# Seven quarter products in place of eight in the second dense layer of the last three token blocks

## The chip, the core and the metric

The kernel runs on one core of one Trainium2 chip. A core has TensorE (matmuls, called PE in the profile; its weight loads are shown apart as PEld), VectorE (DVE), ScalarE (ACT), GpSimd (POOL) and SyncE (SP, which here only issues transfers). [...] Each engine runs its instructions in the order in which they stand in its queue, and waits on semaphores for the others. The metric is the device time of one run of the program in microseconds (us), the median of several runs.

## What is computed

Local and pooled attention over 8 batches of 576 tokens with 8 heads of 64, whose sum is the input x (4608 x 512) of a two-layer block:

```python
def _moe_ref(x, w_in, w_out) -> np.ndarray:
    h = x @ w_in               # 4608 x 512 by 512 x 2048
    g = h - np.tanh(h)
    return (g @ w_out).astype(np.float32)   # 4608 x 2048 by 2048 x 512
```

The attention part, cut: `q`, `k`, `v` are averaged over groups of 4 tokens, attended among themselves and repeated 4 times; to this is added an attention of each token to the tokens less than 4 away; the heads are then joined to the 512 columns of x. The change touches only the last matrix product.

## The kernel before

The attention works on 32 pairs of heads (8 batches of 4 pairs). For each pair q and k are loaded (`qkn`), cast and reordered (`qr`, L408), transposed (`qk`), pooled on GpSimd (`half` L449, `qkd` L454), multiplied to scores (L468 and L484), put through the exponential (`E`, L501 to L514), masked on VectorE (L504, L517), multiplied with v (L528, L535), normalized (`ln`, L546) and transposed back into `xT`, four tiles of 128 x 4608 bf16, one for each 128 columns of x (L572 and L578 for the later batches: the join, on VectorE or GpSimd).

The dense layers work on 9 blocks of 512 tokens. `mm1(kb, fc)` makes one of the 16 groups of 128 hidden columns of block kb: four matmuls of 512 columns (L609) into one of four PSUM slots `ps_hy`, tanh on ScalarE into `u` (L617), the subtraction on VectorE into `gT` (L620, 128 x 16 x 512 bf16, two buffers). `mm2(kb, i)` makes a quarter of an output tile of 128 tokens: four matmuls of 512 columns (L636) with `gT` as the stationary and `w_out_sb` as the moving operand, 16 matmuls for a tile, in the same four PSUM slots. After each fourth call the tile is copied to `y` by ScalarE (L647) and stored by SP (L650, 256 KB). `dense(kb)` interleaves the calls: one `mm1` of block kb, one `mm2` of block kb-1. The last call, `dense(9)`, has only `mm2` of block 8.

The order of work is not that of the program text. Every operation is recorded with its engine, a duration in ns, the keys that it reads and writes, and a priority (a lower number goes first); `Program.order` then plays the program through with these durations and writes each engine's queue in the order of the planned starts. Attention has priorities around 10 times the pair number, tanh, subtraction and copies have -1, the matmuls of the dense layers 5000, so these fill TensorE where attention leaves room. Some operations (casts, pooling, joins) may go to one of several engines and are given to the one that is free first. The real waits are set from the accesses in the resulting order, so the order is fixed while the run's timing is not. In the last part, from about 240 us, attention is over and TensorE has only dense matmuls.

Of the kernel before, what the change touches and what calls it, by code (L numbers as in the profile page):

```python
# [8 lines left out]
FP32 = mybir.dt.float32  # L9
BF16 = mybir.dt.bfloat16  # L10
AF = mybir.ActivationFunctionType
ALU = mybir.AluOpType
# [3 lines left out]
class Program:  # L16
# [18 lines left out]
    def op(self, eng, ns, fn, reads=(), writes=(), pri=0):  # L35
        i = len(self.ops)
        deps = set()
        for key in reads:
            if key in self.last_write:
                deps.add(self.last_write[key])  # L40
        for key in writes:
            if key in self.last_write:
                deps.add(self.last_write[key])
            deps.update(self.readers.get(key, ()))
        for key in reads:
            self.readers.setdefault(key, set()).add(i)
# [104 lines left out]
def kernel(  # L151
# [9 lines left out]
    nc = tc.nc  # L161
    B, H, S, D = q.shape
    Dm, Dff = moe_w_in.shape
# [9 lines left out]
    NT = 5  # L173
    NQ = [120, 120, 120, 120, 96]
    KOFF = 585
    N_FF = Dff // 128
# [6 lines left out]
    def fixed(name, shape, dt, n=None, pool=const):  # L183
        if n is None:
            return pool.tile(shape, dt, name=name, tag=name)
        return [pool.tile(shape, dt, name=f"{name}{i}", tag=f"{name}{i}")
                for i in range(n)]

    NQKN, NVST, NVW = 4, 5, 3
# [4 lines left out]
    xT = [fixed(f"xT{j}", [128, NTOK], BF16) for j in range(NP)]  # L194
    w_in_sb = fixed("w_in_sb", [128, N_DC, Dff], BF16)
    w_out_sb = fixed("w_out_sb", [128, N_FF, Dm], BF16)
    qkn = fixed("qkn", [128, 2, A9 * D], FP32, NQKN)
    vst = fixed("vst", [128, 2, NT, 64], FP32, NVST)
    vw = fixed("vw", [128, 4, NT, 65], BF16, NVW)
    vd = fixed("vd", [128, 2, 4, 65], BF16, NVW)  # L200
    qr = fixed("qr", [128, A9, 128], BF16, 2)
# [2 lines left out]
    half = fixed("half", [128, 2, G, 2], FP32)  # L204
# [7 lines left out]
    r = fixed("r", [128, 2, 7], FP32, 2)  # L212
    ln = fixed("ln", [128, 7, 128], BF16, 2)
    od = fixed("od", [128, G], BF16, 2)
    gT = fixed("gT", [128, N_FF, 512], BF16, 2)
# [3 lines left out]
    ps_ts = fixed("ps_ts", [128, 2, 512], FP32, pool=psum)  # L219
    ps_ox = fixed("ps_ox", [128, 2, 512], FP32, pool=psum)  # L220
# [14 lines left out]
    op = P.op  # L235
    V, A, T, GP = nc.vector, nc.scalar, nc.tensor, nc.gpsimd
# [362 lines left out]
    def mm1(kb, fc):  # L599
        slot, us, g = hy[0] % 4, un[0] % 3, kb % 2  # L600
        hy[0] += 1
        un[0] += 1
        bs = sorted({kb * 512 // S, (kb * 512 + 511) // S})

        def mm(part):
            if not ps_hy:
                dense_banks()
            for dc in range(2 * part, 2 * part + 2):
                T.matmul(ps_hy[slot], w_in_sb[:, dc, fc * 128:(fc + 1) * 128],  # L609
                         xT[dc][:, kb * 512:kb * 512 + 512],  # L610
                         start=(dc == 0), stop=(dc == N_DC - 1))
        for part in range(2):
            op("PE", 432, lambda part=part: mm(part),
               reads=[("w_in", fc // 4, c) for c in range(4)] +
               [("x", b, j) for b in bs for j in range(NP)],
               writes=[("hy", slot)], pri=5000)
        op("ACT", 490, lambda: A.activation(  # L617
            out=u[us], in_=ps_hy[slot], func=AF.Tanh),
           reads=[("hy", slot)], writes=[("u", us)], pri=-1)
        op("DVE", 620, lambda: V.tensor_tensor(  # L620
            out=gT[g][:, fc, :], in0=ps_hy[slot], in1=u[us], op=ALU.subtract),
           reads=[("hy", slot), ("u", us)], writes=[("gT", g, fc)], pri=-1)
# [4 lines left out]
    def mm2(kb, i):  # L627
        ts, part, g = i // 4, i % 4, kb % 2
        if part == 0:
            ycur[0] = hy[0] % 4  # L630
            hy[0] += 1
        slot = ycur[0]

        def mm(e):
            for fc in range(4 * part + 2 * e, 4 * part + 2 * e + 2):
                T.matmul(ps_hy[slot], gT[g][:, fc, ts * 128:ts * 128 + 128],  # L636
                         w_out_sb[:, fc, :],
                         start=(fc == 0), stop=(fc == N_FF - 1))
        for e in range(2):
            op("PE", 432, lambda e=e: mm(e),  # L640
               reads=[("w_out", part, c) for c in range(4)] +
               [("gT", g, fc) for fc in range(4 * part, 4 * part + 4)],
               writes=[("hy", slot)], pri=5000)
        if part == 3:
            ys = yn[0] % 3
            yn[0] += 1
            op("ACT", 490, lambda: A.copy(out=y[ys], in_=ps_hy[slot]),  # L647
               reads=[("hy", slot)], writes=[("y", ys)], pri=-1)
            r0 = kb * 512 + ts * 128
            op("SP", 600, lambda: nc.sync.dma_start(  # L650
                out=out[r0:r0 + 128, :], in_=y[ys]),
               reads=[("y", ys)], writes=[("yq", ys)], pri=-1)
            op("DMA", 1000, None, reads=[("yq", ys), ("y", ys)], pri=-1)

    def dense(kb):

        if kb == 0:
            for i in range(16):
                mm1(kb, i)
            for i in range(M2_FIRST):  # L660
                mm2(kb, i)
            return
        if kb == 1:
            for i in range(16):
                mm1(kb, i)
                if M2_FIRST + i < 16:
                    mm2(0, M2_FIRST + i)
            return
        for i in range(16):
            if kb < NBLK:  # L670
                mm1(kb, i)
            mm2(kb - 1, i)


    M2_FIRST, T_DMA, X_DMA, NEW = 16, 16, 16, 16
# [13 lines left out]
    for i in range(2):  # L689
        def guards(i=i):  # L690
# [3 lines left out]
           writes=[("qk", i, a) for a in range(2)])  # L694
    for i in range(NVW):
        def ones(i=i):
# [3 lines left out]
           writes=[("vd", i), ("vw", i, 0), ("vw", i, 1)])  # L700
        op("POOL", 200, lambda i=i: GP.affine_select(
            out=vd[i][:, 1, :, 64], in_=vd[i][:, 1, :, 64], compare_op=ALU.is_ge,
            fill=0.0, base=-112, pattern=[[0, 4]], channel_multiplier=1),
           writes=[("vd", i)], pri=-96)
    for i in range(2):
        op("DVE", 70, lambda i=i: V.memset(E[i][:, 1728:1840], 0.0),
           writes=[("E", i, 2)], pri=-94)
# [24 lines left out]
    for i in range(2):  # L732
        op("DVE", 70, lambda i=i: V.memset(qkd[i][:, 288:344], 0.0),
           writes=[("qkd", i)], pri=-94)
        op("DVE", 70, lambda i=i: V.memset(vp[i][:, :, :, 64:65], 4.0),
           writes=[("vp", i)], pri=-94)
# [28 lines left out]

    ctx.enter_context(tc.manual_schedule())
# [38 lines left out]
```

## Time and profile before

| | |
|---|---|
| time, median of 3 runs | 343.2 us (343.11 to 343.61) |
| span of the profiled execution | 345.0 us |
| L609, first layer, 576 matmuls of 128x512 | 146.9 us busy |
| L636, second layer, 576 matmuls of 128x512 | 142.7 us busy |
| L620, subtraction on VectorE, 144 | 96.6 us busy, 686 ns each |
| L617, tanh on ScalarE, 144 | 83.9 us busy, 598 ns each |
| L647, copy of an output tile on ScalarE, 36 | 21.2 us busy, 588 ns each |

The profile is of one execution; its span is 1.8 us longer than the median of the timed runs, and every sum made from it is made against 345.0. Busy times of different engines overlap. The busy time of a matmul group is the time in which at least one of them is in flight; the mean duration of one (379 ns) is longer than the distance between two starts, since they are pipelined.

### The profile page before, as it was taken

What the parts mean: (1) busy time and instruction counts of PE and PEld (TensorE: products, weight loads), DVE (VectorE), ACT (ScalarE), POOL (GpSimd) and SP (SyncE); (2) the same over time, 40 slices, a digit from 0 to 9 for tenths busy, and PEclk for the clock granted to TensorE, in tenths of its full rate; (3) what the DMA queues carried; (4) which work ended last, traced back from release to release, by engine and by line L of the source; (5) the groups of instructions that cost most, each with busy time, mean ns of one, the idle gap of its engine ahead of it and who ended that gap; (6) DMA issues with size and microseconds to landing.
All of it is one profiled execution on the core that took longest, in us unless ns stands there. A gap on an engine that the chain in (4) does not pass through costs nothing.

```text
span 345.0 us, 6688 instructions
## 1 busy us (share of the span) xinstructions
PE 326.0 (94%) x2498; PEld 164.2 (48%) x2498; DVE 220.7 (64%) x365; ACT 220.5 (64%) x353; POOL 152.6 (44%) x196
## 2 busy tenths in 40 slices
PE   4978959999999999999899999999999999999995
PEld 1554435555555554444454444544444444444442
DVE  3687747667999977889789777876333433343300
ACT  3775836658997888979878877974443444344411
POOL 5762224555558747987877688462000000000000
PEclk9599989999999999999999999999999999999999
DMA  7999999779869976999999999723001000100021
GB/s 209 240 230 228 206 301 301 195 227 281 219 149 214 244 203 155 246 232 282 233 210 256 234 251 224 105 67 86 30 30 63 30 30 32 61 30 32 31 91 62
DMA packets 99214, 56.52 MB, mean 164 GB/s; under 512 B 77678, under 2 KB 86382, under 8 KB 99182
## 3 DMA queue, kind: packets, MB, share of 16 engines
q1 hardware_dynamic: 94958, 51.91, 61.2%
q0 software_dynamic: 4224, 4.19, 7.3%
q8 instruction: 19, 0.31, 0.4%
q14 instruction: 13, 0.11, 0.1%
HBM read 42.46 MB, written 9.44 MB: 150 GB/s over the span
## 4 chain that ended last, share of the span: by engine, by line
PE 72%; DMA 11%; DVE 4%; ACT 4%; POOL 3%; issue 3%; SPq 1%; POOLq 0%; ACTq 0%; DVEq 0%
PE ps_hy L636 30%; PE ps_hy L609 29%; DMA qkn<-in_k_dram 9%; PE ps_ts L468 3%; PE ps_ox L528 3%; DMA qkn<-in_q_dram 2%; PE ps_ts L433 2%; ACT qk L424 2%; PE ps_ox L535 2%; DVE E L504 2%; PE ps_ox L560 1%; POOL half L449 1%; DVE gT L620 1%; DVE qr L408 1%; POOL v L364 1%
## 5 line engine op out<-in xcount | busy, mean ns | idle before, releaser
L609 PE MATMUL ps_hy<-xT,w_in_sb 128*128 128x512 bf16 x576 | 146.9, 382 | 1.4 <-DVE xT L589 0.9
L636 PE MATMUL ps_hy<-w_out_sb,gT 128*128 128x512 bf16 x576 | 142.7, 379 | 0.0
L620 DVE TENSOR_TENSOR gT<-ps_hy,u 128x512 bf16<-128x512 f32 x144 | 96.6, 686 | 71.4 <-ACT u L617 70.8
L617 ACT ACTIVATE u<-ps_hy 128x512 f32<-128x512 f32 x144 | 83.9, 598 | 69.3 <-PE ps_hy L609 66.7
L636 PEld LDWEIGHTS <-gT 128*128 128x128 bf16 x576 | 54.6, 98 | 63.2
L609 PEld LDWEIGHTS <-w_in_sb 128*128 128x128 bf16 x576 | 53.0, 98 | 61.1 <-issue 3.6
L449 POOL TENSOR_TENSOR half<-qk 128x576 f32<-128x576 bf16 x29 | 33.4, 1151 | 36.9 <-ACT qk L437 26.0
L424 ACT COPY qk<-qT 128x576 bf16<-128x576 bf16 x32 | 37.8, 1206 | 0.0
L546 DVE TENSOR_TENSOR ln<-ps_ox,r 128x896 bf16<-128x896 f32 x32 | 34.9, 1090 | 1.1 <-DVE r L544 0.2
L501 ACT ACTIVATE E<-ps_ts 128x960 bf16<-128x960 f32 x32 | 31.0, 973 | 6.7 <-PE ps_ts L468 6.4
L504 DVE TENSOR_TENSOR E<-E,mask 128x960 bf16<-128x960 bf16 x32 | 28.4, 889 | 10.0 <-ACT E L501 9.7
L647 ACT COPY y<-ps_hy 128x512 f32<-128x512 f32 x36 | 21.2, 588 | 17.0 <-PE ps_hy L636 16.8
L408 DVE CAST qr<-qkn 128x576 bf16<-128x576 f32 x32 | 23.6, 738 | 8.3 <-DMA qkn<-in_k_dram 8.3
L408 POOL CAST qr<-qkn 128x576 bf16<-128x576 f32 x30 | 21.9, 730 | 15.7 <-DMA qkn<-in_k_dram 9.1
L343 POOL CAST vw<-vst 128x640 bf16<-128x640 f32 x30 | 25.3, 844 | 5.8 <-DMA vst<-in_v_dram 5.8
L437 ACT COPY qk<-ps_ts 128x1152 bf16<-128x1152 bf16 x16 | 18.0, 1125 | 10.8 <-PE ps_ts L433 10.5
L528 PE MATMUL ps_ox<-vw,E 128*128 128x65 bf16 x320 | 21.0, 196 | 2.1 <-DVE E L504 0.9
L454 POOL TENSOR_TENSOR qkd<-half 128x288 bf16<-128x288 f32 x30 | 21.2, 705 | 3.6 <-DVE r L544 2.4
L528 PEld LDWEIGHTS <-E 128*128 128x128 bf16 x320 | 17.0, 99 | 9.3 <-DVE E L517 1.4
L364 POOL TENSOR_TENSOR v<-v 72x512 f32<-72x512 f32 x16 | 20.7, 1296 | 0.6
L468 PEld LDWEIGHTS <-qk 64*128 64x128 bf16 x320 | 9.9, 97 | 17.5 <-issue 15.3
L368 POOL TENSOR_TENSOR vp<-v 72x256 bf16<-72x256 f32 x16 | 11.6, 728 | 14.1 <-PE ps_ox L535 14.0
(71 smaller groups left out, 250.0 us busy)
## 6 DMA issues: line engine op xcount, KB each, us to landing
vst<-in_v_dram SPq DMA_DIRECT2D x62, 160.0 KB, 5.2
qkn<-in_q_dram SPq DMA_DIRECT2D x32, 288.0 KB, 4.3
qkn<-in_k_dram SPq DMA_DIRECT2D x32, 288.0 KB, 4.5
out_dram<-y SPq DMA_DIRECT2D x36, 256.0 KB, 4.1
v<-in_v_dram SPq DMA_DIRECT2D x16, 288.0 KB
w_in_sb<-in_moe_w_in_dram POOLq DMA_DIRECT2D x4, 512.0 KB, 12.4
w_out_sb<-in_moe_w_out_dram POOLq DMA_DIRECT2D x4, 512.0 KB, 20.0
vst<-in_v_dram SPq DMA_DIRECT2D x2, 128.0 KB
```

What stands on the lines that cost most here:

```text
L343: P.choice([(eng, ns, lambda fn=fn: fn(out=vw[w][:, 2 * jj:2 * jj + 2, :, 0:64], in_=vst[s])) for eng, ns, fn in CAST_V[p >= NEARLY]], rea ...
L408: P.choice([(eng, ns, lambda dst=dst, srt=srt, fn=fn: fn(out=dst, in_=srt)) for eng, ns, fn in REORDER[p >= NEARLY][h]], reads=[("qkn", sn ...
L424: op("ACT", 600, lambda i=i: A.copy(out=full[:, i].rearrange("p (g a) -> p g a", a=A9), in_=qT[s].rearrange("p a (g i) -> p i g a", i=2)[: ...
L449: eng.tensor_tensor(out=half, in0=four[:, :, :, 0:2], in1=four[:, :, :, 2:4], op=ALU.add)
L501: op("ACT", 870, lambda: A.activation(out=e1, in_=ps[:, :, 0:480], func=AF.Exp, scale=SCALE), reads=ts, writes=[("E", s, 0)], pri=pri)
L504: op("DVE", 700, lambda: V.tensor_tensor(out=e1, in0=e1, in1=mask[:, 0:480].unsqueeze(1).to_broadcast([128, 2, 480]), op=ALU.mult), reads= ...
L528: T.matmul(po[:, hh, 65 * t:65 * t + 65], E[s][:, c:c + 128], vw[w][:, 2 * jj + hh, t, :], start=True, stop=True)
L546: op("DVE", 1010, lambda: V.tensor_tensor(out=ln[s].rearrange("p n (h d) -> p h n d", d=D), in0=blocks[:, :, :, 0:64], in1=r[s].unsqueeze( ...
L609: T.matmul(ps_hy[slot], w_in_sb[:, dc, fc * 128:(fc + 1) * 128], xT[dc][:, kb * 512:kb * 512 + 512], start=(dc == 0), stop=(dc == N_DC - 1))
L617: op("ACT", 490, lambda: A.activation(out=u[us], in_=ps_hy[slot], func=AF.Tanh), reads=[("hy", slot)], writes=[("u", us)], pri=-1)
L620: op("DVE", 620, lambda: V.tensor_tensor(out=gT[g][:, fc, :], in0=ps_hy[slot], in1=u[us], op=ALU.subtract), reads=[("hy", slot), ("u", us) ...
L636: T.matmul(ps_hy[slot], gT[g][:, fc, ts * 128:ts * 128 + 128], w_out_sb[:, fc, :], start=(fc == 0), stop=(fc == N_FF - 1))
```

## The change

For blocks 6, 7 and 8 (`KS = 6`) the product of g (512 tokens x 2048) and w_out (2048 x 512) is cut into quarters, A11 to A22 (256 tokens x 1024) and B11 to B22 (1024 x 256), and the four quarters of the output come from seven products of quarters in place of eight, by the Winograd form of Strassen's scheme. Each product is 16 matmuls of 256 columns (2 halves of 128 tokens, 8 groups of 128 hidden columns), in two steps of 8; a block has 112 of them where it had 64 matmuls of 512 columns.

- `weight_sums` (once, GpSimd, 16 operations of 128x512 bf16, priority 4000): T0 = B12-B11, T1 = B22-T0, T2 = B22-B12, T3 = B21-T1, written over columns 0 to 2047 of the four `xT` tiles, which the first layer has read by then.
- `token_sums` (each block, VectorE, 8 operations of 128x1024 bf16): S2 = A11-A21, S0 = A21+A22, S1 = S0-A11, S3 = A12-S1, written into the `qkn` tiles. The second half of S0 needs the last of the 16 groups of g.
- `phase`: product 1 (A11 B11) and, added into the same bank, 2 (A12 B21); 6 (S1 T1), 7 (S2 T2) and 4 (A22 T3) one after another in a second bank; 5 (S0 T0) and 3 (S3 B22) in a third. The three banks were those of the attention's scores and outputs (`ps_ts`, `ps_ox`). ScalarE copies the bank after 1, 2, 6 and 7 (a running sum, so the bank is not cleared in between); GpSimd adds the copy of 1 to the copies of 6 and 7 (128x512 f32); VectorE adds 5, 4 and 3 to the kept sums, from PSUM, into output tiles of 128 x 2 x 512 that lie over the `vst` buffers. The kept sums lie over `xT`, too.
- An output tile is a half block (256 tokens); its two stores of 256 KB leave together, after 4 and after 3.
- `dense`: in the loop of 16, each `mm1` is followed by one step of the products, in the program's order 1, 5, 6, 7, 2, 4, 3; the planner may move steps. In the planned order of the last block, where there is no first layer left, they stand as 1, 5, 6, 2, 7, 4, 3.
- The five `vst` buffers become slices of one tile of the same size.

```diff
--- before.py
+++ after.py
@@ -195,7 +195,9 @@
     w_in_sb = fixed("w_in_sb", [128, N_DC, Dff], BF16)
     w_out_sb = fixed("w_out_sb", [128, N_FF, Dm], BF16)
     qkn = fixed("qkn", [128, 2, A9 * D], FP32, NQKN)
-    vst = fixed("vst", [128, 2, NT, 64], FP32, NVST)
+    vst_all = fixed("vst", [128, NVST * 2 * NT * 64], FP32)
+    vst = [vst_all[:, 640 * i:640 * i + 640].rearrange("p (h t d) -> p h t d", h=2, t=NT)
+           for i in range(NVST)]
     vw = fixed("vw", [128, 4, NT, 65], BF16, NVW)
     vd = fixed("vd", [128, 2, 4, 65], BF16, NVW)
     qr = fixed("qr", [128, A9, 128], BF16, 2)
@@ -652,6 +654,170 @@
                reads=[("y", ys)], writes=[("yq", ys)], pri=-1)
             op("DMA", 1000, None, reads=[("yq", ys), ("y", ys)], pri=-1)
 
+    KS = 6
+    HB = N_FF // 2
+    HD = Dm // 2
+    bank = [ps_ts[:, 0, :], ps_ts[:, 1, :], ps_ox[:, 0, :]]
+    bkey = [("ts", 0), ("ts", 1), "ox"]
+    Sg = [qkn[i].rearrange("p i n -> p (i n)").bitcast(BF16)[:, 0:HB * 256]
+         .rearrange("p (f c) -> p f c", c=256) for i in range(4)]
+    Tw = [xT[j][:, 0:HB * HD].rearrange("p (f c) -> p f c", c=HD) for j in range(4)]
+    keep = [xT[j][:, 2048:3072].bitcast(FP32) for j in range(3)]
+    y2 = [vst_all[:, 1024 * i:1024 * i + 1024].rearrange("p (j c) -> p j c", j=2)
+          for i in range(3)]
+    tkeys = [("x", bb, j) for bb in range(4) for j in range(4)]
+    def weight_sums():
+        wq = w_out_sb.rearrange("p (r f) (c n) -> p r f c n", r=2, c=2)
+        b11, b12 = wq[:, 0, :, 0, :], wq[:, 0, :, 1, :]
+        b21, b22 = wq[:, 1, :, 0, :], wq[:, 1, :, 1, :]
+        wk = [("w_out", f, c) for f in range(4) for c in range(4)]
+        for n, (x0, x1, k0) in enumerate(((b12, b11, None), (b22, Tw[0], 0),
+                                          (b22, b12, None), (b21, Tw[1], 1))):
+            for e in range(4):
+                fs = slice(2 * e, 2 * e + 2)
+                def go(n=n, x0=x0, x1=x1, fs=fs):
+                    GP.tensor_tensor(out=Tw[n][:, fs], in0=x0[:, fs], in1=x1[:, fs],
+                                     op=ALU.subtract)
+                reads = wk + ([("T", k0, e)] if k0 is not None else [])
...
+                op("POOL", 1100, go, reads=reads, writes=keys, pri=4000)
+    def token_sums(kb):
+        g = kb % 2
+        lo, hi = gT[g][:, 0:HB, :], gT[g][:, HB:, :]
+        a11, a21 = lo[:, :, 0:256], lo[:, :, 256:512]
+        a12, a22 = hi[:, :, 0:256], hi[:, :, 256:512]
+        todo = []
+        for n, x0, x1, sub, k0, h in ((2, a11, a21, 1, None, 0), (0, a21, a22, 0, None, 2),
+                                      (1, Sg[0], a11, 1, 0, 0), (3, a12, Sg[1], 1, 1, 1)):
+            for e in range(2):
+                todo.append((n, x0, x1, sub, k0, h, e))
+        for n, x0, x1, sub, k0, h, e in todo:
+            fs = slice(4 * e, 4 * e + 4)
+            def go(n=n, x0=x0, x1=x1, sub=sub, fs=fs):
+                V.tensor_tensor(out=Sg[n][:, fs], in0=x0[:, fs], in1=x1[:, fs],
+                                op=ALU.subtract if sub else ALU.add)
...
+            op("DVE", 620, go, reads=reads, writes=keys, pri=-1)
+    def phase(kb, n):
+        g = kb % 2
+        wq = w_out_sb.rearrange("p (r f) (c n) -> p r f c n", r=2, c=2)
+        gA = {11: gT[g][:, 0:HB, 0:256], 21: gT[g][:, 0:HB, 256:512],
+              12: gT[g][:, HB:, 0:256], 22: gT[g][:, HB:, 256:512]}
...
+        left, lk, right, rk, bk, first = {
+            1: (gA[11], lo, wq[:, 0, :, 0, :], wkey(0), 0, True),
+            2: (gA[12], hi, wq[:, 1, :, 0, :], wkey(1), 0, False),
+            6: (Sg[1], sk(1), Tw[1], tk(1), 1, True),
+            7: (Sg[2], sk(2), Tw[2], tk(2), 1, False),
+            4: (gA[22], hi, Tw[3], tk(3), 1, False),
+            5: (Sg[0], sk(0), Tw[0], tk(0), 2, True),
+            3: (Sg[3], sk(3), wq[:, 1, :, 1, :], wkey(1), 2, False),
+        }[n]
+        pb = bank[bk].rearrange("p (j c) -> p j c", j=2)
+        key = [bkey[bk]]
+        def mm(e):
+            for j in range(2):
+                for f in range(4 * e, 4 * e + 4):
+                    T.matmul(pb[:, j, :], left[:, f, 128 * j:128 * j + 128],
+                             right[:, f, :], start=(first and e == 0 and j == 0 and f == 0),
+                             stop=(e == 1 and f == HB - 1),
+                             skip_group_check=True)
+        for e in range(2):
+            op("PE", 900, lambda e=e: mm(e), reads=lk[e] + rk, writes=key, pri=5000)
+            yield
+        full = [k.rearrange("p (j c) -> p j c", j=2) for k in keep]
+        ya, yb = y2[(2 * kb) % 3], y2[(2 * kb + 1) % 3]
+        ka, kc = ("y2", (2 * kb) % 3), ("y2", (2 * kb + 1) % 3)
+        def kept(i):
+            return ([("keep", i)] + [("x", bb, i) for bb in (4,)]
+                    if kb == KS else [("keep", i)])
+        if n == 1:
+            op("ACT", 590, lambda: A.copy(out=full[0], in_=pb), reads=key,
+               writes=kept(0), pri=-1)
+        if n == 2:
+            op("ACT", 590, lambda: A.copy(out=ya[:, :, 0:HD], in_=pb), reads=key,
+               writes=[(ka, 0)], pri=-1)
+        if n == 6:
+            op("ACT", 590, lambda: A.copy(out=full[1], in_=pb), reads=key,
+               writes=kept(1), pri=-1)
+            op("POOL", 1150, lambda: GP.tensor_tensor(
+                out=full[1], in0=full[1], in1=full[0], op=ALU.add),
+               reads=[("keep", 0)], writes=[("keep", 1)], pri=-1)
+        if n == 7:
+            op("ACT", 590, lambda: A.copy(out=full[2], in_=pb), reads=key,
+               writes=kept(2), pri=-1)
+            op("POOL", 1150, lambda: GP.tensor_tensor(
+                out=full[2], in0=full[2], in1=full[0], op=ALU.add),
+               reads=[("keep", 0)], writes=[("keep", 2)], pri=-1)
+        if n == 4:
+            op("DVE", 690, lambda: V.tensor_tensor(
+                out=yb[:, :, 0:HD], in0=pb, in1=full[0], op=ALU.add),
+               reads=key + [("keep", 0)], writes=[(kc, 0)], pri=-1)
+        if n == 5:
+            late[0] = lambda: op("DVE", 690, lambda: V.tensor_tensor(
+                out=yb[:, :, HD:], in0=pb, in1=full[2], op=ALU.add),
+                reads=key + [("keep", 2)], writes=[(kc, 1)], pri=-1)
+        if n == 7:
+            late[0]()
+        if n == 4:
+            store(kb, 1, yb, kc)
+        if n == 3:
+            op("DVE", 690, lambda: V.tensor_tensor(
+                out=ya[:, :, HD:], in0=pb, in1=full[1], op=ALU.add),
+               reads=key + [("keep", 1)], writes=[(ka, 1)], pri=-1)
+            store(kb, 0, ya, ka)
+    late = [None]
+    def store(kb, half, t, key):
+        for j in range(2):
+            r0 = kb * 512 + half * 256 + j * 128
+            op("SP", 600, lambda j=j, r0=r0: nc.sync.dma_start(
+                out=out[r0:r0 + 128, :], in_=t[:, j, :]),
+               reads=[(key, 0), (key, 1)], writes=[("yq", key, j)], pri=-1)
+            op("DMA", 1000, None, reads=[("yq", key, j), (key, 0), (key, 1)], pri=-1)
+    def product(kb):
+        for n in (1, 5, 6, 7, 2, 4, 3):
+            yield from phase(kb, n)
     def dense(kb):
 
         if kb == 0:
@@ -666,10 +832,22 @@
                 if M2_FIRST + i < 16:
                     mm2(0, M2_FIRST + i)
             return
+        if kb - 1 == KS:
+            weight_sums()
+        steps = None
+        if kb - 1 >= KS:
+            token_sums(kb - 1)
+            steps = product(kb - 1)
         for i in range(16):
             if kb < NBLK:
                 mm1(kb, i)
-            mm2(kb - 1, i)
+            if steps is None:
+                mm2(kb - 1, i)
+            else:
+                next(steps, None)
+        if steps is not None:
+            for _ in steps:
+                pass
 
 
     M2_FIRST, T_DMA, X_DMA, NEW = 16, 16, 16, 16
```

More of the change, by code (lines that the diff above doesn't have):

```diff
@@ new lines @@
+    y2 = [vst_all[:, 1024 * i:1024 * i + 1024].rearrange("p (j c) -> p j c", j=2)
[14 more added lines that the diff above has]
+                reads = wk + ([("T", k0, e)] if k0 is not None else [])
+                keys = [("T", n, e)]
+                if e == 0:
+                    keys += [("x", bb, n) for bb in range(4)]
+                else:
+                    reads += [("T", n, 0)]
+                op("POOL", 1100, go, reads=reads, writes=keys, pri=4000)
@@ new lines, in token_sums @@
+    def token_sums(kb):
[13 more added lines that the diff above has]
+                                op=ALU.subtract if sub else ALU.add)
+            reads = []
+            if h in (0, 2):
+                reads += [("gT", g, fc) for fc in range(4 * e, 4 * e + 4)]
+            if h in (1, 2):
+                reads += [("gT", g, HB + fc) for fc in range(4 * e, 4 * e + 4)]
+            if k0 is not None:
+                reads.append(("S", k0, e))
+            keys = [("S", n, e)]
+            if kb == KS and e == 0:
+                keys += [("qkn", n, 0), ("qkn", n, 1)]
+            if e == 1:
+                reads.append(("S0", n))
+            else:
+                keys.append(("S0", n))
+            op("DVE", 620, go, reads=reads, writes=keys, pri=-1)
@@ new lines, in phase, with sk, wkey, tk @@
+    def phase(kb, n):
[3 more added lines that the diff above has]
+              12: gT[g][:, HB:, 0:256], 22: gT[g][:, HB:, 256:512]}
+        lo = [[("gT", g, 4 * e + i) for i in range(4)] for e in range(2)]
+        hi = [[("gT", g, HB + 4 * e + i) for i in range(4)] for e in range(2)]
+        def sk(m):
+            return [[("S", m, e)] for e in range(2)]
+        def wkey(r):
+            return [("w_out", 2 * r + e, c) for e in range(2) for c in range(4)]
+        def tk(m):
+            return [("T", m, e) for e in range(4)]
+        left, lk, right, rk, bk, first = {
[60 more added lines that the diff above has]
+            store(kb, 0, ya, ka)
@@ L671, in dense @@
                 mm1(kb, i)
-            mm2(kb - 1, i)
+            if steps is None:
+                mm2(kb - 1, i)
+            else:
+                next(steps, None)
+        if steps is not None:
+            for _ in steps:
+                pass
     M2_FIRST, T_DMA, X_DMA, NEW = 16, 16, 16, 16
```

## The prediction

> **What bounds the kernel now.** I read the head of the page first: busy times, then the granted clock.
>
> ```profile
> span 345.0 us, 6688 instructions
> PE 326.0 (94%) x2498; PEld 164.2 (48%) x2498; DVE 220.7 (64%) x365; ACT 220.5 (64%) x353; POOL 152.6 (44%) x196
> PEclk9599989999999999999999999999999999999999
> ```
>
> TensorE is busy 94% of the span, and after the first few slices its clock is full. [...]
>
> ```profile
> PE 72%; DMA 11%; DVE 4%; ACT 4%; POOL 3%; issue 3%; SPq 1%; POOLq 0%; ACTq 0%; DVEq 0%
> L636 PE MATMUL ps_hy<-w_out_sb,gT 128*128 128x512 bf16 x576 | 142.7, 379 | 0.0
> ```
>
> The chain runs through TensorE for 72%, and L636, the second dense layer, never finds its engine idle. The "mean 379" is latency, not cost: matmuls overlap. The cost is the distance between starts, which I took from the timeline, at the end of the run and at a place with narrower matmuls.
>
> ```profile
> 325.99 14.84 PE L636 MATMUL ps_hy<-w_out_sb,gT 128*128 128x512 bf16 x68
> ...
> 340.91 0.59 ACT L647 COPY y<-ps_hy 128x512 f32<-128x512 f32 x1 [2.87 <-PE ps_hy L636]
> ```
>
> ```profile
> 100.34 0.67 PE L433 MATMUL ps_ts<-ident,qr 128*128 128x128 bf16 x9
> 100.84 0.72 PE L381 MATMUL ps_ox<-vw,pick 128*128 128x256 bf16 x5
> ```
>
> 68 matmuls of 512 columns take 14.84 us; less the last one's latency (0.38) that is 14.46/67 = 0.2158 us each. Nine of 128 columns: (0.67-0.24)/8 = 0.054. Five of 256 columns: (0.72-0.273)/4 = 0.112, where 0.273 is L381's median duration. Each of them loads its own weights, so a load does not set a floor at 0.1. Last, the stretch in which the added weight sums will run, and the waits of TensorE in it (none) against 140 to 200 us:
>
> ```profile
> 205.00:215.00 10.00, 9.91 (x85) 4.75 (x84) 6.55 (x11) 8.23 (x14) 8.51 (x11) 1.00 1.13 211
> 215.00:225.00 10.00, 10.00 (x90) 5.18 (x89) 8.99 (x18) 9.62 (x15) 5.26 (x6) 1.00 0.72 118
> 225.00:235.00 10.00, 9.91 (x85) 4.80 (x84) 7.41 (x12) 7.26 (x13) 4.87 (x7) 1.00 0.31 72
> 235.00:245.00 10.00, 10.00 (x63) 4.85 (x62) 5.09 (x8) 4.05 (x7) 2.64 (x4) 1.00 0.20 52
> ```
>
> ```profile
> PE ps_ox L528 <- DVE E L504: 0.9, 1, 0.9
> PE ps_ox L528 <- DVE E L517: 0.8, 2, 0.5
> PE ps_ox L468 <- DVE ln L546: 0.2, 1, 0.2
> ```
>
> Columns of the windows: length, then busy time of PE, PEld, DVE, ACT, POOL, clock, DMA, GB/s. From 205 us on TensorE has 0.2 us of idle time in 40: the tail of the kernel is a pure stream of matmuls, and what leaves that stream shortens the kernel one for one.
>
> **The change, part by part.** Times are against the profiled execution, 345.0 us; the median of the timed runs is 343.2, so 1.8 comes off at the end. The instruction order of both programs is the same on every engine up to about 205 us; only what follows is priced.
>
> *Matmuls.* Three blocks lose 3 x 64 = 192 matmuls of 512 columns: 192 x 0.2158 = 41.4 us. They gain 3 x 7 x 16 = 336 of 256 columns. Price of one: a straight line between 0.054 (128 columns) and 0.2158 (512) gives 0.108 at 256; the row itself gives 0.112, but its moving operand is four pieces of 64 columns, where the products read 256 in one piece. I take 0.110: 336 x 0.110 = 37.0. Net -4.5, ends -5.1 (0.108) and -3.8 (0.112).
>
> [...]
>
> *Product 7 to product 4, last block.* The block after the last first-layer matmul has nothing to interleave; its order is 1, 5, 6, 2, 7, 4, 3. Products 7 and 4 share a PSUM bank, and 4 may start only when ScalarE has copied 7's sum. From the last matmul's issue to its result: 0.273-0.110 = 0.16; result to copy, 340.83 to 340.91 in the tail above: 0.08; copy 0.59 (L647); ScalarE's end to the next engine's start, 326.79 to 326.82 in L617 and L620: 0.03. Stall +0.86; it cannot be hidden, ends 0.8 and 1.0. Behind the waiting matmul stand 4 and 3, so all that is left.
>
> *Product 4 to product 3.* Bank of 5 and 3: VectorE must first add 5 to keep[2], which waits for GpSimd's add on the copy of 7. Chain from 7's last issue: 0.83 to the copy's end, 0.03, GpSimd add of 128x512 f32, 0.03, VectorE add 0.69 (L620's form, PSUM and f32), 0.03. GpSimd's nearest rows: 1.15 (L449, 576 columns) and 1.27 (L364, 512 columns f32; longest 1.74). I take 1.27, the same operation: 2.88. TensorE arrives after 0.86 + 16 x 0.110 = 2.62. Stall +0.26, ends 0.1 and 0.7.
>
> *Last eviction and stores.* A VectorE add (0.69) replaces the copy (0.59): +0.10. Then two stores of 256 KB leave together where one left. One issue takes 0.33 us on SP; one store's data took 0.83 (its packets in the trace, 342.33 to 343.16; the window 342.3 to 343.2 has 291 GB/s, 262 KB). If the data go one after the other: +0.83; if they overlap fully, only the second issue: +0.38. I take 0.83, as one store already uses all 16 engines at 0.77. The other half's two stores leave 2 us earlier and are through by then.
>
> *Interleaved stretch (blocks 6 and 7).* Between products stand first-layer matmuls: 6 x 0.216 = 1.30 before 7, 4 x 0.216 = 0.86 before 2 and before 4. In the order of instructions with their waits, product 2 waits for ScalarE as well as 4, so both waits can be for the copy just before: 0.86 against 0.86, no slack, in 4 places. A tanh in the way (0.60) would add that much. I take +0.1 in all, ends 0 and 2.4 (4 x 0.60).
>
> *Sums of quarters on VectorE.* 24 of 128x1024 bf16; L504 (960 columns, two bf16 inputs) takes 0.66 undisturbed, 2.16 at worst beside GpSimd. At 0.70 a block needs 16 x 0.69 (L620) + 8 x 0.70 + 3 x 0.69 = 18.7 us of the 26 it has: hidden. In the tail the last of S0 is ready 1.52 (last L609 issue 325.99 to the end of its L620, 327.51) + 0.03 + 0.70 = 2.25 after the last first-layer matmul; product 5's second half wants it at 24 x 0.110 = 2.64. Price 0; without that 0.4 us of cover, at 2.16 an instruction, up to 1.1.
>
> *Weight sums on GpSimd.* 16 of 128x512 bf16: L572 (480 columns) 1.012, so 1.08, 17.3 us in all, placed between the attention steps of the last pairs; three joins of xT (L572 and L578, 1.36 each) go to VectorE for it. From 205 to 245 us GpSimd goes from 21.3 of 40 to 21.3 + 17.3 - 4.1 = 34.5, 86%. In 140 to 200 us, where it is at 80% (48.1 of 60), TensorE waited 1.9 us on VectorE behind the exp masks; by that 40 us cost 1.3. Against it: qkd was ready 3.5 to 4 us before the score matmuls here (L454 ends 228.61, scores start 232.11). Between 0 and 1.3 I take +0.5; a gain is excluded, there are 0.2 us of idle time to win. The first dense block that needs the sums starts near 271, 25 us after they end.
>
> Removed beside this: 12 copies of L647 on ScalarE, replaced by 12 of the same size; 12 stores stay 12. Priced at nothing, because ScalarE is idle a fifth of that stretch and more.
>
> Sum: -4.5 + 0.86 + 0.26 + 0.10 + 0.83 + 0.1 + 0.5 = -1.85. Span 343.15, less 1.8: **341.4 us**.
>
> **Rivals.** *A: the gain goes into the copies between products.* If the tanhs stand in front of the copies in the four places, +2.4 - 0.1: 343.7, no measurable change. For it: zero slack. Against: the tanh before each copy belongs to a first-layer group that ended 0.88 earlier, and takes 0.60.
>
> *B: slower, through GpSimd.* The weight sums push qkd and the masked exponentials of the last four pairs behind the fixed order of TensorE; the longest such wait is the 0.9 us shown above. One for each: 3.6, less the 0.5 already counted: 344.5. It decides from 3.0 us of added stalls, which make 343.9. For it: 86% load on an in-order engine; the masks reach 2.16 beside GpSimd. Against: slack of 3.5 us on qkd.
>
> *C: it does not do what it says.* A pair of load and 256-column matmul that keeps up only 0.120 over hundreds, not five, gives 336 x 0.120 = 40.3: -1.1 in place of -4.5, 344.8. Against: 128 columns at 0.054 with loads.
>
> **How the numbers follow.** About 0.2% (0.7 us) is what a measurement of this kernel can tell from no change: below 342.5 is faster, above 343.9 slower. Forecast 0.70, A 0.16, B 0.10, C 0.04: faster 0.70, same 0.16, slower 0.14. Range: all cheap ends give -5.1 + 0.8 + 0.1 + 0.1 + 0.38 = -3.7, 339.5, unlikely together, so 339.8; upwards it takes in A and stops at 343.9, leaving B and C out.
>
> **What would show it.** The new matmuls start 0.108 to 0.112 apart; in the last block one gap near 0.9 in front of product 4 and a smaller one in front of 3; the last two stores' data 0.8 one after the other; weight sums done near 245 and TensorE idle under 1 us between 205 and 245. Wrong would be: gaps in front of products 2, 4 or 7 while first-layer matmuls run (A), in front of scores or outputs of the last pairs (B), or starts 0.12 apart (C).

## The result and the profile after

The changed kernel takes 359.8 us (median of four runs, 354.8 to 360.8) against 343.3 us, where 341.4 was forecast and 343.9 was the end of the range. A run over 1.5% above the fastest of its kernel counts as slow and stays out of the ratio (here 360.5 and 360.8, in the last experiment 345.3): by the other two runs the ratio is 1.040, 95% interval 1.033 to 1.046. It is slower by 4%, and by nearly 5% if all four count. The profiled execution has a span of 357.4 us where the kernel before had 345.0. The head of its page:

```profile
span 357.4 us, 6994 instructions
PE 321.2 (90%) x2599; PEld 179.4 (50%) x2642; DVE 260.9 (73%) x406; ACT 221.1 (62%) x353; POOL 174.2 (49%) x210
...
PE 64%; DVE 12%; DMA 7%; ACT 5%; issue 5%; POOL 3%; SPq 2%; POOLq 0%; ACTq 0%; DVEq 0%
```

TensorE is busy for 4.8 us less than before (321.2 against 326.0), VectorE for 40 us more, in which long waits inside an instruction count as busy (one addition below counts for 5.26 us). Of the chain of waits, VectorE has 12% where it had 4%. The stretch from 200 to 260 us in windows, columns as before (length; PE, PEld, DVE, ACT, POOL; clock; DMA; GB/s):

```profile
200.00:210.00 10.00, 9.69 (x76) 4.63 (x78) 7.74 (x10) 8.23 (x13) 8.91 (x9) 1.00 1.25 227
210.00:220.00 10.00, 4.94 (x28) 2.04 (x25) 8.54 (x9) 3.45 (x6) 4.13 (x5) 0.83 0.31 68
220.00:230.00 10.00, 9.41 (x73) 4.54 (x71) 8.17 (x11) 8.04 (x13) 8.44 (x8) 1.00 0.29 51
230.00:240.00 10.00, 6.75 (x42) 3.20 (x44) 6.64 (x8) 2.82 (x5) 8.02 (x9) 0.66 0.19 49
240.00:250.00 10.00, 6.17 (x37) 2.75 (x38) 8.40 (x9) 2.14 (x5) 4.28 (x4) 0.83 0.06 12
250.00:260.00 10.00, 9.94 (x74) 5.03 (x75) 6.50 (x11) 5.09 (x9) 1.73 (x2) 1.00 0.30 78
```

In three of the six windows TensorE stands still for 3 to 5 us, and in the same three the clock is at 0.66 to 0.83. Narrower windows, laid behind each of the three stalls, show the clock at one half:

```profile
215.10:218.40 3.30, 3.10 (x13) 1.20 (x13) 2.65 (x6) 0.87 (x2) 0.00 (x0) 0.50 0.36 70
232.10:238.90 6.80, 5.65 (x37) 2.71 (x39) 3.50 (x7) 1.54 (x2) 4.83 (x6) 0.50 0.22 51
245.80:249.10 3.30, 3.08 (x20) 1.58 (x19) 2.35 (x5) 0.00 (x0) 0.00 (x0) 0.50 0.00 0
```

TensorE is busy for 11.8 us in them. Four matmuls of the first layer took 1.91 us there (from 216.57) where four took 1.03 at a clock of 1.00 (from 261.40), so by estimate half of it, 5.9 us, is lost. Whom TensorE waited for between 200 and 260 us (total, times, longest):

```profile
PE ps_ox L470 <- DVE ln L548: 5.1, 1, 5.1
PE ps_ox L530 <- DVE E L519: 3.8, 2, 3.3
PE ps_ox L530 <- DVE E L506: 3.1, 1, 3.1
```

12.0 us on VectorE, where the kernel before waited for nothing in the same stretch. (The lines are numbered two higher than before: L506 is the mask of the exponentials, L548 the normalization, L574 and L580 the join of xT, L622 the subtraction; L681 is a weight sum, L706 a token sum, L757 a product's matmul.) The timeline of GpSimd and then of VectorE at the first of these stalls shows why:

```profile
208.51 1.68 POOL L366 TENSOR_TENSOR v<-v 72x512 f32<-72x512 f32 x1
210.16 1.14 POOL L451 TENSOR_TENSOR half<-qk 128x576 f32<-128x576 bf16 x1
211.26 1.14 POOL L681 TENSOR_TENSOR xT<-w_out_sb 128x512 bf16<-128x512 bf16 x1
212.37 0.66 POOL L456 TENSOR_TENSOR qkd<-half 128x288 bf16<-128x288 f32 x1
212.99 1.14 POOL L681 TENSOR_TENSOR xT<-w_out_sb 128x512 bf16<-128x512 bf16 x1
...
208.99 5.26 DVE L580 TENSOR_TENSOR xT<-lT 128x96 bf16<-128x96 bf16 x1
214.17 1.08 DVE L548 TENSOR_TENSOR ln<-ps_ox,r 128x896 bf16<-128x896 f32 x1
```

A VectorE addition of 96 columns, 0.24 us at its shortest, takes 5.26 us: it ends 0.1 us after the last of five GpSimd instructions that follow one another without a gap (212.99 + 1.14 = 214.13; after that GpSimd is idle). Behind it in VectorE's queue stands L548, and TensorE's scores wait for that. At 238.96 us a mask (L506, 0.64 at its shortest) takes 5.84 us: it begins in the fourth of eight weight sums in a row and waits for that one and four more. GpSimd, then VectorE:

```profile
235.37 4.48 POOL L681 TENSOR_TENSOR xT<-w_out_sb 128x512 bf16<-128x512 bf16 x4
239.81 4.47 POOL L681 TENSOR_TENSOR xT<-w_out_sb,xT 128x512 bf16<-128x512 bf16 x4
...
238.96 5.84 DVE L506 TENSOR_TENSOR E<-E,mask 128x960 bf16<-128x960 bf16 x1 [1.06 <-ACT E L503]
```

Between these two lies a third run of GpSimd instructions without a gap, from 223.39 to 232.09, and there VectorE gets in. Again GpSimd, then VectorE:

```profile
223.39 1.26 POOL L366 TENSOR_TENSOR v<-v 72x512 f32<-72x512 f32 x1
224.61 0.66 POOL L456 TENSOR_TENSOR qkd<-half 128x288 bf16<-128x288 f32 x1
225.23 5.75 POOL L681 TENSOR_TENSOR xT<-w_out_sb,xT 128x512 bf16<-128x512 bf16 x4
230.95 1.14 POOL L451 TENSOR_TENSOR half<-qk 128x576 f32<-128x576 bf16 x1
...
223.75 2.04 DVE L574 TENSOR_TENSOR xT<-lT 128x480 bf16<-128x480 bf16 x1
...
227.44 1.01 DVE L506 TENSOR_TENSOR E<-E,mask 128x960 bf16<-128x960 bf16 x1
...
229.90 2.31 DVE L580 TENSOR_TENSOR xT<-lT 128x96 bf16<-128x96 bf16 x1
```

The join at 223.75 and the mask at 227.44 end while the four sums go on, and the four take 5.75 us where four took 4.48 above. So a VectorE operation with two inputs from the on-chip memory (the tiles without `ps_` in their names) waited for one GpSimd instruction in some rows (the mask of 1.01 us, 0.64 at its shortest) and for several in others; the longest waits, 5.26 and 5.84 us, lasted to the end of a run, but not every run was waited out. What decides this stays open.

The account of the 12.4 us between the spans has to start with the profile of the kernel before. That execution was itself a late one: where both are on record, a span is 1.7 to 2.0 us below the time of its run, so that 345.0 belongs to a run of about 346.7 and not to the median of 343.2. The subtractions on VectorE (L620, now L622), 144 in either trace, serve as milestones. Start in us of subtraction number:

| | 11 | 21 | 76 | 96 |
|---|---|---|---|---|
| before | 42.18 | 86.99 | 202.72 | 243.94 |
| changed | 41.94 | 82.44 | 198.11 | 257.91 |
| difference | -0.24 | -4.55 | -4.61 | +13.97 |

The profiled execution of the kernel before lost 4.6 us near 45 us from the start, where the two programs are still the same (TensorE is busy for 6.31 us from 40 to 50 us, in the changed kernel for 8.81, and from 48.9 to 52.3 us the clock before is 0.50). From number 76 to number 96, the stage with the weight sums, the changed kernel then takes 59.8 us where the kernel before took 41.2: the stage lost 18.6 us. 12.0 of these are the waits, and about 5.9 the half clock behind them.

By the spans, block 6's second layer starts at 285.57 where it started at 271.60, which is +14.0 = 18.6 - 4.6. From there to the end of the last matmul's issue it is 67.1 us where it was 69.1, -2.0; this holds the matmuls saved and the waits of the last block, shown here in the timeline of TensorE (in brackets the idle time before):

```profile
342.89 1.04 PE L757 MATMUL ps_ts<-w_out_sb,gT 128*128 128x256 bf16 x8
344.61 1.03 PE L757 MATMUL ps_ts<-w_out_sb,gT 128*128 128x256 bf16 x8 [0.67 <-ACT xT L778]
345.48 1.04 PE L757 MATMUL ps_ts<-xT,qkn 128*128 128x256 bf16 x8
347.19 1.03 PE L757 MATMUL ps_ts<-xT,qkn 128*128 128x256 bf16 x8 [0.67 <-ACT vst L775]
348.89 1.91 PE L757 MATMUL ps_ts<-xT,gT 128*128 128x256 bf16 x16 [0.67 <-ACT xT L784]
350.96 1.91 PE L757 MATMUL ps_ox<-w_out_sb,qkn 128*128 128x256 bf16 x16 [0.16 <-DVE vst L794]
```

Start to start, 343.66 to 344.61, 346.24 to 347.19 and 347.95 to 348.89, these are three gaps of 0.95 us, 0.84 more than the 0.11 of a matmul, and one of 0.43. They stand in the middle of product 2, in the middle of 7, and in front of 4 and 3. After the last matmul's issue come 4.7 us where it was 4.3, +0.4.

### The profile page after: what moved, and what is told of

Read it like the earlier page. It is cut to its first block, busy times and chain, and to the rows that moved or that the text cites. A ratio compares the mean times of both kernels' runs of the same rounds, so it can differ in the third digit from the quotient of the medians.

```text
span 357.4 us, 6994 instructions
## 1 busy us (share of the span) xinstructions
PE 321.2 (90%) x2599; PEld 179.4 (50%) x2642; DVE 260.9 (73%) x406; ACT 221.1 (62%) x353; POOL 174.2 (49%) x210
## 4 chain that ended last, share of the span: by engine, by line
PE 64%; DVE 12%; DMA 7%; ACT 5%; issue 5%; POOL 3%; SPq 2%; POOLq 0%; ACTq 0%; DVEq 0%
PE ps_hy L611 26%; PE ps_hy L638 17%; PE ps_ts L757 6%; DMA qkn<-in_k_dram 6%; DVE E L506 4%; PE ps_ox L757 3%; DVE xT L580 3%; PE ps_ox L530 2%; PE ps_ts L470 2%; DVE gT L622 2%; PE ps_ts L435 2%; PE ps_ox L537 2%; DVE xT L574 2%; ACT qk L426 1%; SPq L318 1%
## 5 line engine op out<-in xcount | busy, mean ns | idle before, releaser
L611 PE MATMUL ps_hy<-xT,w_in_sb 128*128 128x512 bf16 x550 | 145.0, 385 | 3.8 <-issue 1.3
L619 ACT ACTIVATE u<-ps_hy 128x512 f32<-128x512 f32 x144 | 84.8, 598 | 76.8 <-PE ps_hy L611 72.8
L622 DVE TENSOR_TENSOR gT<-ps_hy,u 128x512 bf16<-128x512 f32 x144 | 97.1, 686 | 48.2 <-ACT u L619 47.0
L638 PE MATMUL ps_hy<-w_out_sb,gT 128*128 128x512 bf16 x370 | 97.0, 384 | 1.6 <-issue 1.2
L638 PEld LDWEIGHTS <-gT 128*128 128x128 bf16 x384 | 36.0, 99 | 40.8 <-issue 2.1
L451 POOL TENSOR_TENSOR half<-qk 128x576 f32<-128x576 bf16 x29 | 33.3, 1149 | 47.2 <-ACT qk L439 26.7
L780 POOL TENSOR_TENSOR xT<-xT,xT 128x512 f32<-128x512 f32 x3 | 3.8, 1267 | 81.3 <-ACT xT L778 81.3
L506 DVE TENSOR_TENSOR E<-E,mask 128x960 bf16<-128x960 bf16 x32 | 34.3, 1074 | 11.5 <-ACT E L503 11.2
L548 DVE TENSOR_TENSOR ln<-ps_ox,r 128x896 bf16<-128x896 f32 x32 | 34.9, 1089 | 1.1 <-DVE r L546 0.2
L757 PEld LDWEIGHTS <-qkn 128*128 128x128 bf16 x192 | 18.8, 98 | 6.8 <-issue 1.2
## 6 DMA issues: line engine op xcount, KB each, us to landing
w_in_sb<-in_moe_w_in_dram POOLq DMA_DIRECT2D x4, 512.0 KB, 11.8
```

What stands on the lines that cost most here:

```text
L451: eng.tensor_tensor(out=half, in0=four[:, :, :, 0:2], in1=four[:, :, :, 2:4], op=ALU.add)
L506: op("DVE", 700, lambda: V.tensor_tensor(out=e1, in0=e1, in1=mask[:, 0:480].unsqueeze(1).to_broadcast([128, 2, 480]), op=ALU.mult), reads= ...
L548: op("DVE", 1010, lambda: V.tensor_tensor(out=ln[s].rearrange("p n (h d) -> p h n d", d=D), in0=blocks[:, :, :, 0:64], in1=r[s].unsqueeze( ...
L619: op("ACT", 490, lambda: A.activation(out=u[us], in_=ps_hy[slot], func=AF.Tanh), reads=[("hy", slot)], writes=[("u", us)], pri=-1)
L622: op("DVE", 620, lambda: V.tensor_tensor(out=gT[g][:, fc, :], in0=ps_hy[slot], in1=u[us], op=ALU.subtract), reads=[("hy", slot), ("u", us) ...
L757: T.matmul(pb[:, j, :], left[:, f, 128 * j:128 * j + 128], right[:, f, :], start=(first and e == 0 and j == 0 and f == 0), stop=(e == 1 an ...
```

## The experiments

Theory L: GpSimd instructions that read the on-chip memory and follow one another without a gap keep a VectorE operation with two inputs from that memory out until the run ends. (The third run above already shows that "until the run ends" is too strong; the experiments ask whether it is the reading that keeps VectorE out.) Theory Q: GpSimd's queue is too full, so pooling and joins are late. Theory S: the products, the token sums or the new places of the buffers cost the time. For the last block, theory P: waits are set by PSUM tile (the `ps_` tiles) and not by bank.

**Weight sums held back until after the attention**

```diff
                 reads = wk + ([("T", k0, e)] if k0 is not None else [])
+                reads += [("x", 7, j) for j in range(4)]
```

> The changed kernel with its 16 GpSimd weight sums held back until the last join of xT, so that they run after the attention. Theory L (lockout: while GpSimd runs instructions back to back, a VectorE operation with two SBUF inputs can't proceed, and TensorE waits for it): the stalls between 205 and 250 us go. What is left of the changed kernel's account is -4.7 (matmuls), +2.8 (waits in the last block) and +0.4 (last stores): 343.3 - 1.5 = 341.8, range 341 to 343. Theory Q (GpSimd's queue is late with pooling and joins): the same time, since its load during attention goes too. Theory S (the products, the sums on VectorE or the new buffers themselves cost the time): stays near 356.

Measured 342.35 us beside 344.06 of the kernel before, ratio 0.996 (0.993 to 0.999). In its trace TensorE has no wait for VectorE between 200 and 250 us, and GpSimd works through the sums from 238 to 257 us, behind the last join:

```profile
230.00:240.00 10.00, 9.95 (x63) 4.81 (x63) 5.44 (x9) 4.32 (x10) 4.28 (x6) 1.00 0.31 72
240.00:250.00 10.00, 9.95 (x47) 4.54 (x47) 4.06 (x6) 4.12 (x8) 10.00 (x10) 1.00 0.14 53
```

S falls: products, token sums and buffers are as in the changed kernel, and the loss has become a gain of 1.7 us, the size that the account leaves (-2.0 + 0.4). What costs the time is where the sums stand.

**Weight sums on VectorE**

```diff
-                    GP.tensor_tensor(out=Tw[n][:, fs], in0=x0[:, fs], in1=x1[:, fs],
+                    V.tensor_tensor(out=Tw[n][:, fs], in0=x0[:, fs], in1=x1[:, fs],
...
-                op("POOL", 1100, go, reads=reads, writes=keys, pri=4000)
+                op("DVE", 420, go, reads=reads, writes=keys, pri=4000)
```

> The changed kernel with the 16 weight sums on VectorE, at the same priority and so at about the same place between the attention steps. Theory L: no run of GpSimd instructions, so no operation over 2.2 us on VectorE; 16 x 0.4 us more VectorE work in the stage costs 0 to 3 us of TensorE: 342 to 345. Theory Q: GpSimd's queue is as before, so 342 to 345 as well. Theory S: near 356.

Measured 347.9 us, ratio 1.011 (1.008 to 1.015): 12 us less than with the sums on GpSimd, but outside the expected 342 to 345. VectorE is now busy for 9.96 and 10.0 of 10 us in 210 to 230, and TensorE waits 2.7 us for it there, most of the 1.5 us that it is idle in each of these two windows. The long operations are gone: from 200 us on the longest with two inputs from the on-chip memory is a sum itself, 1.85 us beside GpSimd where the shortest sum took 0.41.

**The sums alone, in the kernel before**

```diff
+        if kb - 1 == KS:
+            weight_sums()
         for i in range(16):
             if kb < NBLK:
                 mm1(kb, i)
             mm2(kb - 1, i)
```

> The kernel before with nothing added but the 16 GpSimd weight sums at the same place; their results are not used, the second layer is the old one. Theories L and Q: the whole loss of that stage without any gain of the products, 343.3 + 12 to 15 = 355 to 358, with VectorE operations of 5 us between 205 and 250 us. Theory S: 343 to 344.

Measured 362.5 us, ratio 1.053 (1.048 to 1.058), a loss of 18.5 us, more than expected. The 16 additions alone, 18 us of work on an engine that is idle half of the time, cost more than the whole change, whose products win some 2 us back. The same stalls stand in the trace: a join of 96 columns took 5.26 us (L578 at 209.74) and a mask 6.38 (L504 at 239.19), both to the end of a run of GpSimd.

**The sums spread out**

```diff
+                i = 4 * n + e
+                reads += [("gT", 1, i)]
...
+                    GP.tensor_copy(out=tick[0:1, 0:1], in_=gT[1][0:1, 4 * n + fs.start // 2, 0:1])
                     GP.tensor_tensor(out=Tw[n][:, fs], in0=x0[:, fs], in1=x1[:, fs],
```

> The changed kernel with the same 16 GpSimd sums in the same stage, but each behind a copy of one element that waits for a VectorE result, so that GpSimd has a gap between two sums. GpSimd's load is the same or a little more. Theory L: VectorE gets in at each gap, no operation over 2.2 us, stalls of TensorE in the stage fall from 14 to below 4: 342 to 346. Theory Q (load and order of the queue): the stalls stay, 352 to 358.

Measured 348.75 us, ratio 1.014 (1.008 to 1.020): between the two expectations. The edit did not do what it was to do. Where the copy's wait was already met, no gap opened; GpSimd, then VectorE:

```profile
230.76 0.18 POOL L682 COPY tick<-gT 1x1 bf16<-1x1 bf16 x1
230.90 1.14 POOL L683 TENSOR_TENSOR xT<-w_out_sb,xT 128x512 bf16<-128x512 bf16 x1
231.99 0.18 POOL L682 COPY tick<-gT 1x1 bf16<-1x1 bf16 x1
232.13 1.14 POOL L683 TENSOR_TENSOR xT<-w_out_sb,xT 128x512 bf16<-128x512 bf16 x1
233.23 0.18 POOL L682 COPY tick<-gT 1x1 bf16<-1x1 bf16 x1
233.36 1.14 POOL L683 TENSOR_TENSOR xT<-w_out_sb,xT 128x512 bf16<-128x512 bf16 x1
235.93 0.48 POOL L682 COPY tick<-gT 1x1 bf16<-1x1 bf16 x1 [1.42 <-DVE gT L623]
...
231.00 4.02 DVE L507 TENSOR_TENSOR E<-E,mask 128x960 bf16<-128x960 bf16 x1 [0.92 <-ACT E L504]
```

The mask lasts until the run ends (233.36 + 1.14 = 234.50) and then takes its own half microsecond. So an instruction that waits for something long done does not break a run. Runs were shorter than in the changed kernel (up to 7.9 us where it has 9.1, 8.7 and 10.2), the longest operation was shorter (4.05 against 5.84), and so was the loss; a full queue (Q) is not excluded by this one.

**Memsets in place of the sums** (the sums are left out, so the last three blocks are not the reference's)

```diff
-                    GP.tensor_tensor(out=Tw[n][:, fs], in0=x0[:, fs], in1=x1[:, fs],
-                                     op=ALU.subtract)
+                    GP.memset(Tw[n][:, fs], 0.0)
+                    GP.memset(Tw[n][:, fs], 0.0)
```

> The changed kernel with each of the 16 GpSimd weight sums replaced by two memsets of the same 128x512 bf16 target (the sums are left out, the products of the last three blocks multiply zeros for them). A memset of 576 columns took 0.58 us, so GpSimd is loaded about as long, in the same places of its queue, but reads nothing. Theory L (a run of GpSimd instructions that read the on-chip memory keeps a VectorE operation with two such inputs out): VectorE operations stay below 2.2 us and TensorE's stalls between 205 and 250 us fall below 4 us: 341 to 346. Theory Q (the load and order of GpSimd's queue): 352 to 360 as with the sums.

Measured 342.8 us, ratio 0.998 (0.995 to 1.000). GpSimd is as full as with the sums (33.3 of 40 us in 200 to 240), its queue has the same order with two memsets for each sum, and VectorE passes beside it; GpSimd, then VectorE:

```profile
220.88 0.52 POOL L682 MEMSET xT<- 128x512 bf16 x1
221.34 0.52 POOL L681 MEMSET xT<- 128x512 bf16 x1
...
221.00 0.64 DVE L506 TENSOR_TENSOR E<-E,mask 128x960 bf16<-128x960 bf16 x1
```

No wait of TensorE for VectorE in the stage is left, and no operation with two inputs from the on-chip memory took over 1.35 us there, though GpSimd's runs last up to 10.8 us (gaps of 0.06 us between memsets not counted). Q falls: the same load and order, written and not read, cost 0.6 of the 18.6 us. Of L it is shown that runs of instructions that read kept VectorE out (a mask of 5.84 us) where runs that only write did not (0.64); a memset is also shorter than a sum (0.52 against 1.14), and the two are not told apart here. That the wait lasts until the run ends holds for the longest waits alone. In the trace of each run, subtraction 76 to 96 took 41.2 us with the late sums, 44.9 with the sums on VectorE, 61.0 with the sums alone, 49.8 with them spread, and 41.8 with the memsets.

**Banks of three tiles in the last block** (on top of the late sums)

```diff
-        pb = bank[bk].rearrange("p (j c) -> p j c", j=2)
-        key = [bkey[bk]]
+        last = kb == NBLK - 1
+        key = [[("ts", 0), "ox", ("hy", 0)][bk] if last else bkey[bk]]
+
+        def pb():
+            own = [ps_ts[:, 0, :], ps_ox[:, 0, :], ps_hy[0]] if last else bank
+            return own[bk].rearrange("p (j c) -> p j c", j=2)
```

> The kernel with the late sums; in the last block products 1 and 2, products 6, 7 and 4, and products 5 and 3 use banks of three different PSUM tiles (in the others 1, 2 share a tile of two banks with 6, 7, 4). Theory P (waits are set by tile, so a copy out of one bank waits for a product in the other bank, and the next product for the copy): of the three gaps of 0.95 us in the last block two go and the one between 7 and 4 stays: 2 x 0.84 = 1.7 us less than with the late sums, span about 338.4, time 340.6. Rival (ScalarE's copies are late for another reason): all three stay, 342.

Measured 341.1 us, ratio 0.992 (0.989 to 0.995), beside 0.996 with the late sums alone in another set of runs. Two of the three gaps are gone, the one in front of product 4 is there unchanged:

```profile
327.20 1.91 PE L762 MATMUL ps_ts<-w_out_sb,gT 128*128 128x256 bf16 x16
328.95 1.91 PE L762 MATMUL ps_ox<-xT,qkn 128*128 128x256 bf16 x16
331.53 1.91 PE L762 MATMUL ps_ox<-xT,gT 128*128 128x256 bf16 x16 [0.67 <-ACT xT L789]
```

P stands by these gaps (the times alone, 0.992 against 0.996, would not show it): with 1, 2 and 6, 7, 4 in the two banks of one tile, the copy of 6 waited for the half of 2 that stood before it in the order, and the other half of 2 for the copy.

**The order of the last block** (on top of that)

```diff
+        if kb == NBLK - 1:
+            six, five = phase(kb, 6), phase(kb, 5)
+            for step in (phase(kb, 1), six, five, phase(kb, 7), phase(kb, 2),
+                         phase(kb, 4), phase(kb, 3)):
...
```

> As with the banks of three tiles, and the last block's order is 1, 6 and 5 in halves by turns, first half of 2, 7, second half of 2, 4, 3, so that another half product stands between 6 and 7 and between 7 and 4. If the copy (0.85 us from a product's last matmul to the next product's first) is all that holds 4 back, the gap of 0.84 us shrinks below 0.1, and the one in front of 3 (0.32) stays or shrinks: span about 337.6, time 339.8, and a ratio to the kernel before near 0.988. If another wait comes in its place, no faster than with the banks alone.

Measured 338.8 us beside 343.5, ratio 0.985 (0.982 to 0.988), a little below the expected 339.8: faster than both kernels, by 4.7 us against the one before. The last block runs through with one gap of 0.40 us left, in front of product 3:

```profile
327.12 1.91 PE L762 MATMUL ps_ox<-xT,qkn 128*128 128x256 bf16 x16
328.87 1.04 PE L762 MATMUL ps_ts<-w_out_sb,gT 128*128 128x256 bf16 x8
329.74 1.91 PE L762 MATMUL ps_ox<-xT,gT 128*128 128x256 bf16 x16
331.78 1.91 PE L762 MATMUL ps_hy<-w_out_sb,qkn 128*128 128x256 bf16 x16
```

## Why the prediction was wrong

The step that failed is *Weight sums on GpSimd*: "by that 40 us cost 1.3 ... Between 0 and 1.3 I take +0.5". In its stage it measured +18.6, of which 12.0 are waits for VectorE and about 5.9 matmuls at half the clock behind them. The bound was made from GpSimd's share of busy time, 80% against 86%, as if a wait grew with the load. With the same load of memsets the stage lost 0.6 (41.8 against 41.2). What cost the time here were GpSimd instructions that read the on-chip memory, one right behind another, while VectorE had an operation with two such inputs on TensorE's path (the join of 5.26 us and the mask of 5.84).

Unbroken runs alone would not have told me the size. The kernel before has them too, up to 6.7 us with eight instructions at 136.8 us, and its worst mask, 2.16 us at 154.03, got in behind two instructions of a run. From 200 us on its runs last up to 4.9 us; the sums, which have nothing to wait for, filled the gaps and made runs of 9.1, 8.7 and 10.2. Two of these were waited out at 5.26 and 5.84 us, the third was not. The order of GpSimd's queue, with the sums in rows, was there to be read, and so was the row that told two cases apart: L504 reached 2.16 while L620, of the same engine but with one input from PSUM, never passed 0.694 in 144.

The change also put more such operations on VectorE. The prediction counts three joins that move there from GpSimd; it was four (L572 stands on GpSimd 9 times before, L574 5 times after). Beside the memsets the same four stand on VectorE and the stage lost 0.6 in all, so the move by itself costs little.

Rival B named GpSimd, and the stage and the waiting matmuls were its own; its size (0.9 us for each of four pairs) came from the longest wait seen at 80% load, the same wrong measure. Against it I had set the 3.5 us by which qkd is early. Qkd was never late: the waits came through VectorE's masks and joins, which had no such slack.

The rest, by its terms. *Matmuls*: 0.109 us each, -4.7 against -4.5 forecast; that the products save what they should was right. *Product 7 to 4*: 0.84, forecast 0.86. *4 to 3*: 0.32, forecast 0.26. *Missed*: two more gaps of 0.84 in the middle of products 2 and 7. I had seen that 2 waits for ScalarE, and priced it only for the interleaved blocks, at 0.1; not seen was that the copy itself waits for the first half of the product in the other bank, so that the covering half product could not cover. *Interleaved stretch*: no wait of TensorE from 260 us to the last block, 0 against 0.1; rival A did not come. *Token sums*: 0.69 each and hidden, as forecast (0.70). *Last eviction and stores*: +0.4 against 0.93; two stores' data took 1.52 us where one took 0.83, near the 1.66 forecast for one after the other, but from the end of the data to the end of the span it was 1.4 us where it was 1.8. Rival C fell with the 0.109.

The sum was set against the span of 345.0, with 1.8 to come off at the end. That was an execution late by 4.6 us in a part that the change leaves alone; the differences summed here are not touched by it.

With the failed step at 0 and the two missed gaps in, the sum is -4.7 + 0.84 + 0.32 + 1.68 + 0.4 = -1.5; the kernel with the late sums measured -1.7.

## What to carry to other kernels

Work for an engine with idle time had a price here, since another engine's operations waited for it: 16 GpSimd sums that read the on-chip memory and had nothing to wait for cost 18.5 us among the attention's masks and joins; with the sums behind the last join, the same stage took 41.2 us, as in the kernel before. So that is where they belong in this kernel, and the first thing to look for in another is a VectorE operation with two inputs from that memory, on the path, beside such a run. Load shares and the length of GpSimd's runs did not give the price in these traces: memsets at 33.3 of 40 us lost 0.6, and a run of 8.7 us was not waited out where 9.1 and 10.2 were, for 5.26 and 5.84. A planner with durations alone sees a free engine there. Two profiles are two executions: before a difference of spans is put down to a change, milestones that both traces have show where it arose. When a PSUM tile holds more than one bank, look in the order of instructions for a copy of one bank between two halves of a product in the other (here two gaps of 0.84 us).

## What the runs showed of the hardware

In the changed kernel a VectorE addition of 96 columns took 5.26 us and a mask of 960 columns 5.84, with the sums alone a mask took 6.38, each until a run of GpSimd instructions ended. In other places of the changed kernel's trace a join (2.04) and a mask (1.01) got in between two instructions of a run without a gap, and four GpSimd sums took 5.75 there where four took 4.48. A GpSimd instruction whose wait was already met (the 0.18 us copies) did not break a run: beside it a mask took 4.02. Beside memsets a mask took its 0.64. Subtractions with an input from PSUM never passed 0.694 us in 144, in the kernel before and in the changed one. Behind stalls of 3 to 5 us the granted clock of TensorE was 0.50 for 3.4 to 6.8 us (215.0 to 218.4, 232.1 to 238.9 and 245.7 to 249.1 in the changed kernel); in the same stage it was 1.00 where no stall stood (200 to 210, 220 to 230, 250 to 260). Matmuls of 256 columns with a weight load each kept 0.109 us from start to start, where nothing held them, over the 336 of them (16 in 1.91 us, of which the last one's own 0.273).
